# A fused linear-attention and mixture-of-experts kernel: other banks and engines for the first two half batches, plain loads for four v tiles, and a new written order

## The chip, the cores and the metric

The kernel runs on one core of a Trainium2 chip. The core has a matrix engine (TensorE, PE in the profile, with PEld for its weight loads), a vector engine (VectorE, DVE), an activation engine (ScalarE, ACT), a general one (GpSimd, POOL) and a queue engine (SyncE, SP), and 16 DMA engines that SP's, POOL's and ACT's transfers share. The metric is the device time of one execution in microseconds. Three runs before the change took 956.26, 956.44 and 956.66 us; the median, 956.44, is what the change is compared with.

## The reference, cut to what matters

```python
# q, k, v: (8, 8, 576, 64) float32; moe: x (4608, 512), w_gate (512, 8), w1 (8, 512, 1024), w2 (8, 1024, 512)
def phi(x): return np.where(x > 0, x, np.exp(x) - 1.0) + 1.0
q_p, k_p = phi(q), phi(k)
kv = einsum('bhsd,bhse->bhde', k_p, v);  z = sum(k_p, axis=2)
num = einsum('bhsd,bhde->bhse', q_p, kv)
den = einsum('bhsd,bhd->bhs', q_p, z)[..., None] + 1e-06
x = (num / den) transposed to (4608, 512)

P = exp(x @ w_gate - max)
for _ in range(8):                       # Sinkhorn: rows, then columns
    P /= P.sum(1, keepdims=True) + 1e-09
    P /= P.sum(0, keepdims=True) + 1e-09
    P *= N / E
out = sum over the experts e of P[:, e:e+1] * (maximum(x @ w1[e], 0) @ w2[e])
```

Every token goes through all eight experts, so nearly all of the arithmetic is in the two matrix products per expert.

## The kernel before, in words

**Two stages.** The front computes the attention and leaves its result x, turned (features on the partitions), in the fp16 tile xT. The experts follow: expert 0 with plain products (layer 1 at L618 with its relu at L622, layer 2 at L886), started while the front still runs, so that TensorE has work between the small attention products; the last four token groups of expert 0 and all of experts 1 to 7 with a seven-product scheme (L764/L769 for layer 1, L1024 for layer 2). There are nine groups g of 512 tokens. Layer 1 of a group has eight column blocks f0 to f7 of 128 columns of w1, each a sum over four chunks c of 128 features. For g = 0 the blocks f0 to f3 first do chunks 0 and 1, which half batch 0 yields, and later chunks 2 and 3, which half batch 1 yields.

**The front, by half batches.** `att(b, g)` handles four heads of one batch; there are 16 such half batches, n = 2b + g. Each has these steps:

- loads of k, q (one tile of two, `kqin`) and v (`vin`), L290, each tile with two buffers; for n = 0 and 1 on SP's queue, for n = 2 to 5 all on POOL's, from n = 6 on k and q on SP's and v on POOL's. `VC` is the set of half batches whose v is cast to fp16 by its load: from n = 2 on
- phi as max(x + 1, 1) at L319 (called t) and the minimum of that with exp at L322 (m) on VectorE, and exp at L306 on ScalarE
- v copied into a tile with a column of ones (the helper `copy`, L255 on ScalarE and L257 on VectorE)
- kv, 18 products (L351), and its scaled copy z (L363 on ScalarE, L365 on VectorE)
- q turned by TensorE (qT, L381) and copied out of PSUM
- num, in two parts of three and two row blocks (L407): the numerators, and the denominators as a further column. Then add 1e-6 (L417 on ScalarE, L419 on VectorE), the reciprocal (L422), and the quotient xn (L425, VectorE alone)
- xn turned by TensorE (xT, L440) and copied into the tile xT

Logits (L461) follow every two batches.

**PSUM.** The pool `kvps` has two pairs of banks, the tile `kv_ps`; kv, qT, num, xT and the logits all take turns in it. The pool `hqp` has two single banks, the tile `hq`, for layer 1 (blocks f0, f1, f4, f5, ... in turn; f2 and f3 of the first group use the two banks of layer 2). A bank is free again once its reader has run: for `hq`, the relu at L622.

**What sets the order.** The class `_Plan` takes tasks with costs, dependences and buffer groups. A written list, `order`, then gives for every engine and queue the numbers of its tasks in the order in which they are issued, up to the start of expert 1; behind that the planner picks by its costs. Each engine runs its tasks in that order and waits where an input or a buffer isn't ready. The costs in the code do not make the kernel wait; they only steer the planner where no list is written.

**The start.** SP issues the six loads of n = 0 and 1. POOL waits for v of n = 0 with a small copy, the gate (L342), then issues w1 of expert 0 in two halves, the loads of n = 2 and 3, w2 in two halves, and n = 4 and 5. TensorE runs 38 products on a tile of zeros (L536, `f_warm`): 30 tasks of one and four of two.

Of the kernel before, what the change touches and what calls it, by code (L numbers as in the profile page):

```python
# [11 lines left out]
FP16 = mybir.dt.float16  # L12
# [127 lines left out]
def kernel(  # L140
# [46 lines left out]
    VC = range(2, 2 * B)  # L187
# [19 lines left out]
    p_kv = S_.pool(2)  # L207

# [63 lines left out]
    def att(b, g):  # L272
# [6 lines left out]
        for nm, ten in (("k", k), ("q", q), ("v", v)):  # L279
# [17 lines left out]
            tin[nm] = fadd(("dma", 1.5 if n < 2 else 1.7), lambda _: None, deps=[ti], use=[gr], prio=pr, lat=2.6)  # L297
# [39 lines left out]
        tvv.append(fadd({"act": 1.15, "dve": 0.4 if n in VC else 0.76}, f_v, deps=[ta, tin["v"]],  # L337
# [36 lines left out]
        for j0, j1 in ((0, 5), (5, NJ)) if n < 2 else ((0, NJ),):  # L374
            gp = S_.grp(p_kv)

            def f_qt(_, gp=gp, j0=j0, j1=j1):
                gp["tile"] = pair_tile(FP16).rearrange("p b t -> p (b t)")[:, 0:(j1 - j0) * 2 * PW].rearrange(
                    "p (j h w) -> p j h w", h=2, w=PW)
                for j in range(j0, j1):  # L380
                    nc.tensor.transpose(gp["tile"][:, j - j0].rearrange("p h w -> p (h w)"),  # L381
                                        gt["q"]["tile"][:, j, 2:4, :].rearrange("p r d -> p (r d)"), ident)
# [15 lines left out]
        for i0, i1 in ((0, 3), (3, 5)):  # L398
# [25 lines left out]
            def f_xn(_, num=num, grd=grd, i0=i0, i1=i1, ni=ni):  # L424
                nc.vector.tensor_tensor(  # L425
                    out=gxn["tile"][:, i0:i1].rearrange("p i r h e -> p h (i r) e"), in0=num()[:, :, :, 0:D],
                    in1=grd["tile"][:, :, 0:2 * ni, None].broadcast_to([P, 2, 2 * ni, D]), op=ALU.mult)
# [4 lines left out]
            txn.append(fadd(("dve", 0.95 if ni == 3 else 0.69), f_xn, deps=[t2, txa], use=[gn, grd, gxn], prio=pr))  # L432
        for c0, c1 in ((0, 1), (1, 2)) if n < 2 else ((0, 2),):
            gx = S_.grp(p_kv)

            def f_xt(_, gx=gx, c0=c0, c1=c1):
                gx["tile"] = pair_tile(FP16)
                for c2 in range(c0, c1):
                    for i in range(5):
                        nc.tensor.transpose(gx["tile"][:, c2, 64 * js[i]:64 * js[i] + P],  # L440
                                            gxn["tile"][:, i, c2].rearrange("p h e -> p (h e)"), ident)

            def f_xc(e, gx=gx, c0=c0, c1=c1):
                copy(e, xT[:, 2 * g + c0:2 * g + c1, S * b:S * b + S], gx["tile"][:, c0:c1, 0:S])
# [89 lines left out]
    def f_warm(_, n=1):  # L534
        for _ in range(n):
            nc.tensor.matmul(yw[0], lhsT=warm[:, 0:P], rhs=warm, start=True, stop=True)  # L536
# [6 lines left out]
    for i in range(34):  # L543
        twa = add(("pe", 0.43 if i < 16 else 0.22), lambda e, n=2 if 12 <= i < 16 else 1: f_warm(e, n), deps=[twa],
# [10 lines left out]
    for b in range(1, B):  # L555
        att(b, 0)
        att(b, 1)
        if b == 1:
            w_t[0] += load_w2(0, prio=-96.5, parts=2, deps=[in_prev[0]])
# [562 lines left out]
    for d, k_ in zip(chain, chain[1:]):  # L1122
# [4 lines left out]
        485 515 525 573 1561 1563 1565 576 1083 1570 1567 1081 1107 1109 1206 1572 1574 1204 1230 1576 1232 1327 1329  # L1127
        1353
        pe 2 3 4 5 6 7 8 9 10 11 12 13 14 15 16 17 56 18 54 19 51 20 59 21 22 23 63 24 25 26 85 27 90 88 67 28 69 93
# [17 lines left out]
        sp 36 38 40 71 73 75 237 239 267 269 299 301 329 331 359 361 389 391 421 423 451 453 581 481 595 483 588 511  # L1147
        513 590 602 604 583 609 999 611 597 789 1001 791 1003 1005 1007 1009 1011 893 841 1122 843 1124 1126 945 895
        1128 947 1130 1132 1134 1245 1247 1249 1251 1253 1255 1257 1368 1370 1372 1374 1376 1378 1380 1491 1493 1495
        1497  # L1150
        act 42 43 49 77 52 78 84 64 116 117 619 621 625 627 146 629 147 128 631 623 633 155 165 161 183 184 169 642
# [11 lines left out]
        dve 44 45 46 47 57 79 55 80 81 60 61 82 62 65 66 86 91 89 68 70 94 95 98 96 99 100 102 104 118 120 119 121 123  # L1163
# [15 lines left out]
        dma 37 39 41 72 74 76 107 109 111 113 115 141 143 145 172 174 178 180 182 208 210 212 238 240 242 268 270 272  # L1179
# [39 lines left out]
```

## Time and profile before

| | |
|---|---|
| median of three runs | 956.44 us (956.26 to 956.66) |
| the profiled execution's own time | 956.11 us |
| its span, first to last instruction | 954.3 us |
| mean granted TensorE clock | 1.000 |
| TensorE busy | 944.9 us, 99% |
| VectorE, ScalarE, GpSimd busy | 770.4, 565.9, 161.2 us |
| load of k or q, SP's queue, issue to landing | 6.2 and 7.3 us (median), 576 KB each |
| load of k or q, POOL's queue | 10.3 and 11.3 us, 576 KB each |
| load of v with cast, POOL's queue | 8.3 us, 288 KB written |
| exp of k or q, L306 | 1.17 us, 128x1152 |
| t from fp32, L319, VectorE | 0.75 us, 128x1152 |
| copy of v on VectorE, fp16 to fp16 | 0.45 us; on ScalarE 1.15 us from fp32 |
| copy of qT, 128x1152 | 0.76 us on VectorE, 1.13 us on ScalarE |

How to read it: the profile is of one execution. A line such as "L306 ACT ACTIVATE e<-kqin" gives the source line, the engine, the operation and the tiles written and read. The name behind an arrow in brackets at the end of a line of the timeline is what ended the engine's idle time before it. TensorE's products overlap, so its busy time also holds products whose start is 0.216 us after the one before and whose record is 0.379 us long; gaps are best read from start to start.

### The profile page before, as it was taken

What the parts mean: (1) busy time and instruction counts of PE and PEld (TensorE: products, weight loads), DVE (VectorE), ACT (ScalarE), POOL (GpSimd) and SP (SyncE); (2) the same over time, 40 slices, a digit from 0 to 9 for tenths busy, and PEclk for the clock granted to TensorE, in tenths of its full rate; (3) what the DMA queues carried; (4) which work ended last, traced back from release to release, by engine and by line L of the source; (5) the groups of instructions that cost most, each with busy time, mean ns of one, the idle gap of its engine ahead of it and who ended that gap; (6) DMA issues with size and microseconds to landing.
All of it is one profiled execution on the core that took longest, in us unless ns stands there. A gap on an engine that the chain in (4) does not pass through costs nothing.

```text
span 954.3 us, 18433 instructions
## 1 busy us (share of the span) xinstructions
PE 944.9 (99%) x7096; PEld 643.8 (67%) x7096; DVE 770.4 (81%) x1528; ACT 565.9 (59%) x1024; POOL 161.2 (17%) x209
## 2 busy tenths in 40 slices
PE   8999999999999999999999999999999999999998
PEld 4565676466676667766676666766677666766676
DVE  7898988788887787888887787977877788877776
ACT  5799764765555555555555555555555555555551
POOL 4211000112112211221112211221112211111111
PEclk9999999999999999999999999999999999999999
DMA  9998783634255422544135431644125431425545
GB/s 305 276 252 224 197 252 117 100 78 99 68 149 111 112 67 61 112 111 100 57 115 113 102 89 45 147 105 107 57 67 108 111 98 56 139 78 160 151 105 133
DMA packets 110456, 117.67 MB, mean 123 GB/s; under 512 B 7840, under 2 KB 96544, under 8 KB 110368
## 3 DMA queue, kind: packets, MB, share of 16 engines
q1 hardware_dynamic: 81600, 90.33, 31.0%
q0 software_dynamic: 28368, 25.64, 16.6%
q8 instruction: 55, 0.90, 0.4%
q10 hardware_dynamic: 400, 0.52, 0.2%
q14 instruction: 33, 0.27, 0.1%
HBM read 119.69 MB, written 17.69 MB: 144 GB/s over the span
## 4 chain that ended last, share of the span: by engine, by line
PE 95%; DMA 2%; DVE 1%; ACT 1%; issue 0%; SPq 0%; DVEq 0%; ACTq 0%
PE ye L1024 34%; PE hq L764 20%; PE att L764 10%; PE ye L886 6%; PE Zye L1024 6%; PE Zye L764 5%; PE hq L769 4%; PE hq L618 3%; PE att L769 2%; DMA kqin<-in_k_dram 2%; PE Zye L769 1%; PE kv_ps L440 1%; PE kv_ps L351 1%; PE kv_ps L407 1%; PE kv_ps L381 1%; ACT e L306 1%
## 5 line engine op out<-in xcount | busy, mean ns | idle before, releaser
L1038 DVE SCALAR_TENSOR_TENSOR acc<-ye,P_sb,acc 128x256 f32<-128x256 f32 x620 | 266.5, 477 | 105.8 <-PE ye L1024 104.0
L1024 PEld LDWEIGHTS <-S 128*128 128x128 f16 x1984 | 194.1, 98 | 45.9 <-issue 0.2
L1048 POOL TENSOR_TENSOR acc<-acc,h 128x256 f32<-128x256 f32 x124 | 103.2, 849 | 603.3 <-ACT h L1045 603.2
L1024 PE MATMUL ye<-h,S 128*128 128x256 f16 x1488 | 192.8, 273 | 0.0
L1024 PEld LDWEIGHTS <-h 128*128 128x128 f16 x1488 | 145.6, 98 | 40.0 <-issue 0.2
L804 ACT ACTIVATE h<-hq 128x512 f16<-128x512 f32 x134 | 80.1, 598 | 139.5 <-PE hq L764 122.2
L764 PEld LDWEIGHTS <-W 128*128 128x128 f16 x896 | 87.7, 98 | 81.2
L764 PE MATMUL hq<-xs,W 128*128 128x512 f16 x448 | 133.2, 379 | 0.0
L764 PE MATMUL att<-xs,W 128*128 128x512 f16 x448 | 133.2, 379 | 0.0
L764 PE MATMUL hq<-xs,w 128*128 128x512 f16 x448 | 124.1, 379 | 0.4 <-DVE h L807 0.4
L764 PEld LDWEIGHTS <-w 128*128 128x128 f16 x672 | 65.8, 98 | 55.2 <-issue 0.6
L807 DVE CUSTOM_DVE_ANT_0 h<-att,s 128x512 f16<-128x512 f32 x126 | 86.5, 686 | 20.3 <-ACT s L791 19.8
L801 ACT ACTIVATE h<-Zye 128x512 f16<-128x512 f32 x134 | 80.2, 598 | 32.0 <-PE Zye L764 26.3
L784 ACT COPY Zye<-hq 128x512 f32<-128x512 f32 x134 | 77.7, 580 | 32.3 <-PE hq L764 23.1
L1045 ACT ACTIVATE h<-Zye,P_sb 128x256 f32<-128x256 f32 x124 | 52.4, 471 | 74.7 <-PE Zye L1024 74.5
L791 ACT COPY s<-hq 128x512 f32<-128x512 f32 x126 | 73.5, 584 | 35.3 <-PE hq L764 30.9
L807 DVE CUSTOM_DVE_ANT_0 h<-hq,s 128x512 f16<-128x512 f32 x126 | 86.4, 685 | 9.8 <-PE hq L764 9.3
L995 DVE TENSOR_TENSOR S<-h 128x1024 f16<-128x1024 f16 x124 | 85.3, 688 | 6.2 <-ACT h L804 6.2
L798 ACT COPY s<-att 128x512 f32<-128x512 f32 x126 | 74.5, 591 | 0.9 <-PE att L764 0.9
L886 PE MATMUL ye<-w,h 128*128 128x512 f16 x296 | 73.1, 379 | 0.0
L764 PE MATMUL Zye<-xs,w 128*128 128x512 f16 x224 | 66.6, 379 | 0.0
L1024 PE MATMUL ye<-h,h 128*128 128x256 f16 x496 | 64.3, 273 | 0.0
(121 smaller groups left out, 1077.0 us busy)
## 6 DMA issues: line engine op xcount, KB each, us to landing
xs<-xd SPq DMA_DIRECT2D x196, 256.0 KB, 4.0
w<-in_moe_w_dram POOLq DMA_DIRECT2D x48, 256.0 KB, 4.1
out_dram<-acc SPq DMA_DIRECT2D x67, 128.0 KB, 2.4
kqin<-in_k_dram SPq DMA_DIRECT2D x12, 576.0 KB, 6.2
kqin<-in_q_dram SPq DMA_DIRECT2D x12, 576.0 KB, 7.3
xs<-xd SPq DMA_DIRECT2D x49, 128.0 KB, 2.5
vin<-in_v_dram POOLq DMA_DIRECT2D x14, 288.0 KB, 8.3
xd<-xT SPq DMA_DIRECT2D x27, 128.0 KB, 3.4
```

The costliest lines, as they stand in the source:

```text
L764: nc.tensor.matmul(dst, lhsT=lhs(0, c), rhs=X(b)(c), start=(first and c == 0), stop=(c == 1), skip_group_check=True)
L784: nc.scalar.copy(out=Zt[1], in_=gX["tile"])
L791: nc.scalar.copy(out=gs2["tile"], in_=gX["tile"])
L798: nc.scalar.copy(out=gs5["tile"], in_=gR["tile"])
L801: nc.scalar.activation(out=hd(0, 0), in_=Zt[1], func=AF.Relu)
L804: nc.scalar.activation(out=hd(1, 0), in_=gX["tile"], func=AF.Relu)
L807: nc.vector._custom_dve(TENSOR_ADD_SAT, out=dst, in0=ps, in1=sb, s0=3.0e38, s1=0.0)
L886: nc.tensor.matmul(gy[tt]["tile"], lhsT=hx(f, P * tt, P), rhs=gw2["tile"][:, f, :], start=(f == 0), stop=(f == NFT - 1))
L995: nc.vector.tensor_tensor(out=gS[i]["tile"], in0=a0, in1=a1, op=op)
L1024: nc.tensor.matmul(bank(g_)[:, s, :], lhsT=lhs(s, kk), rhs=rhs(kk), start=(new and s == 0 and kk == 0), stop=(kk == 3), skip_group_check=True)
L1038: nc.vector.scalar_tensor_tensor(out=dst(), in0=bank(g_)[:, s, :], scalar=P_sb[:, gg, e:e + 1], in1=dst(), op0=ALU.mult, op1=ALU.add)
L1048: nc.gpsimd.tensor_tensor(out=dst(), in0=dst(), in1=gst["tile"], op=ALU.add)
```

## The change

It does five things; SP's and POOL's lists keep their first 30 us as they were.

- qT of half batches 0 and 1, and xT of half batch 0, are written to the single banks of `hqp` (`bank_tile`) and no longer to pairs of `kvps`. xT of half batch 1 stays in `kvps`.
- For half batches 0 and 1 `f_xn` can also run on ScalarE, as one multiply by the reciprocal for each row block and head (128x64 each). The order uses it once: for the two-block part of half batch 1, eight multiplies.
- `VC` starts at 6: v of half batches 2 to 5 comes as fp32, and the copy into the tile with the ones does the cast. These loads stay on POOL's queue.
- The 34 warm-up tasks have one product each: 34 in all. 17 of them are ahead of the first qT, where there were 20 products.
- The written order is new for all engines. At the front: VectorE does m of q ahead of m of k for n = 0; ScalarE takes the add of n = 0's three-block part (behind the cast of v, n = 1), both copies of qT n = 1, and one of the two copies of each xT of n = 0 and 1; VectorE takes the add of the two-block part. On TensorE the two-block num comes ahead of the three-block one, and num of n = 2 (two blocks) ahead of qT and kv of n = 3. VectorE takes the copies of qT n = 2 and xT n = 3, and z n = 3, from ScalarE; ScalarE takes the copies of v n = 3 and 5 and of xT n = 2. Further back TensorE has kv of half batch 14 right behind that of 13, and other tasks change between VectorE and ScalarE. The first load of w2 no longer depends on the last of n = 3's loads in the planner's eyes; POOL's list has it in the same place.

The planner's costs for loads and copies also change.

```diff
-    VC = range(2, 2 * B)
+    VC = range(6, 2 * B)
...
+    def bank_tile():
+        return hqp.tile([P, 1024], FP16, tag="hq", name="hq")
...
-            gp = S_.grp(p_kv)
+            gp = S_.grp(p_hq if n < 2 else p_kv)
...
-                gp["tile"] = pair_tile(FP16).rearrange("p b t -> p (b t)")[:, 0:(j1 - j0) * 2 * PW].rearrange(
-                    "p (j h w) -> p j h w", h=2, w=PW)
+                tl = bank_tile() if n < 2 else pair_tile(FP16).rearrange("p b t -> p (b t)")
+                gp["tile"] = tl[:, 0:(j1 - j0) * 2 * PW].rearrange("p (j h w) -> p j h w", h=2, w=PW)
...
-            def f_xn(_, num=num, grd=grd, i0=i0, i1=i1, ni=ni):
+            def f_xn(eng, num=num, grd=grd, i0=i0, i1=i1, ni=ni):
+                if eng == "act":
+                    for m in range(2 * ni):
+                        for h in range(2):
+                            nc.scalar.mul(out=gxn["tile"][:, i0 + m // 2, m % 2, h, :], in_=num()[:, h, m, 0:D],
+                                          mul=grd["tile"][:, h, m:m + 1])
+                    return
...
-            gx = S_.grp(p_kv)
+            gx = S_.grp(p_hq if n == 0 else p_kv)
...
-    def f_warm(_, n=1):
-        for _ in range(n):
-            nc.tensor.matmul(yw[0], lhsT=warm[:, 0:P], rhs=warm, start=True, stop=True)
+    def f_warm(_):
+        nc.tensor.matmul(yw[0], lhsT=warm[:, 0:P], rhs=warm, start=True, stop=True)
...
-            w_t[0] += load_w2(0, prio=-96.5, parts=2, deps=[in_prev[0]])
+            w_t[0] += load_w2(0, prio=-96.5, parts=2)
```

The order's first numbers on ScalarE and VectorE:

```diff
-        act 42 43 49 77 52 78 84 64 116 117 619 621 625 627 146 629 147 128 631 623 633 155 165 161 183 184 169 642
+        act 42 43 49 77 52 78 84 60 91 89 68 100 102 116 117 619 621 623 627 146 629 147 153 631 633 625 165 161 139
...
-        dve 44 45 46 47 57 79 55 80 81 60 61 82 62 65 66 86 91 89 68 70 94 95 98 96 99 100 102 104 118 120 119 121 123
+        dve 44 46 47 45 55 79 57 80 81 64 65 82 66 61 62 86 70 98 99 94 95 96 104 118 120 119 121 123 148 128 149 150
```

Here 116 and 117 are the exps of k and q for n = 2, 619, 621, ... the relus of layer 1's first group, 100 the part of xn n = 1, 91 and 89 the copies of qT n = 1, 68 and 102 copies of xT.

More of the change, by code (lines that the diff above doesn't have):

```diff
@@ L296, in att @@
             in_prev[0] = ti
-            tin[nm] = fadd(("dma", 1.5 if n < 2 else 1.7), lambda _: None, deps=[ti], use=[gr], prio=pr, lat=2.6)
+            tin[nm] = fadd(("dma", 1.55 if n < 2 else 2.0 if nm == "v" and n in VC else 1.7), lambda _: None, deps=[ti], use=[gr], prio=pr, lat=2.6)
         ge, gtt = S_.grp(p_e), S_.grp(p_t)
@@ L336, in f_v @@
             copy(e, gvv["tile"][:, :, :, 0:D], gin["v"]["tile"])
-        tvv.append(fadd({"act": 1.15, "dve": 0.4 if n in VC else 0.76}, f_v, deps=[ta, tin["v"]],
+        tvv.append(fadd({"act": 1.15, "dve": 0.46 if n in VC else 0.76}, f_v, deps=[ta, tin["v"]],
                         use=[gvv, gin["v"]], prio=pr))
@@ L431, in att @@
             t2 = fadd(("dve", 0.22), f_rd, deps=[t2], use=[grd], prio=pr)
-            txn.append(fadd(("dve", 0.95 if ni == 3 else 0.69), f_xn, deps=[t2, txa], use=[gn, grd, gxn], prio=pr))
+            txn.append(fadd({"dve": 0.95 if ni == 3 else 0.69, **({"act": 0.8 * ni} if n < 2 else {})}, f_xn, deps=[t2, txa], use=[gn, grd, gxn], prio=pr))
         for c0, c1 in ((0, 1), (1, 2)) if n < 2 else ((0, 2),):
-            gx = S_.grp(p_kv)
+            gx = S_.grp(p_hq if n == 0 else p_kv)
             def f_xt(_, gx=gx, c0=c0, c1=c1):
-                gx["tile"] = pair_tile(FP16)
+                gx["tile"] = bank_tile()[:, None, :] if n == 0 else pair_tile(FP16)[:, 0:c1 - c0]
                 for c2 in range(c0, c1):
                     for i in range(5):
-                        nc.tensor.transpose(gx["tile"][:, c2, 64 * js[i]:64 * js[i] + P],
+                        nc.tensor.transpose(gx["tile"][:, c2 - c0, 64 * js[i]:64 * js[i] + P],
                                             gxn["tile"][:, i, c2].rearrange("p h e -> p (h e)"), ident)
             def f_xc(e, gx=gx, c0=c0, c1=c1):
-                copy(e, xT[:, 2 * g + c0:2 * g + c1, S * b:S * b + S], gx["tile"][:, c0:c1, 0:S])
+                copy(e, xT[:, 2 * g + c0:2 * g + c1, S * b:S * b + S], gx["tile"][:, :, 0:S])
             t1 = fadd(("pe", 0.28 * (c1 - c0)), f_xt, deps=txn, acq=[gx], use=[gxn], prio=pr)
@@ L543 @@
     for i in range(34):
-        twa = add(("pe", 0.43 if i < 16 else 0.22), lambda e, n=2 if 12 <= i < 16 else 1: f_warm(e, n), deps=[twa],
+        twa = add(("pe", 0.43 if i < 26 else 0.22), f_warm, deps=[twa],
                   use=[gyw], prio=900.0, after=1.2 + 0.43 * min(i, 16) + 0.55 * max(i - 16, 0))
@@ L1126 @@
         pool 0 50 106 108 110 112 114 140 142 144 171 173 177 179 544 181 207 209 211 241 271 303 333 363 393 425 455
-        485 515 525 573 1561 1563 1565 576 1083 1570 1567 1081 1107 1109 1206 1572 1574 1204 1230 1576 1232 1327 1329
-        1353
-        pe 2 3 4 5 6 7 8 9 10 11 12 13 14 15 16 17 56 18 54 19 51 20 59 21 22 23 63 24 25 26 85 27 90 88 67 28 69 93
[12 rows of a table removed]
+        485 515 525 576 573 1561 1081 1570 1563 1572 1574 1565 1109 1107 1083 1567 1230 1206 1576 1204 1232 1327 1329
+        1353 1355
+        pe 2 3 4 5 6 7 8 9 10 11 12 13 14 15 16 17 18 56 54 19 51 20 21 22 63 59 23 24 25 88 90 26 27 85 28 29 67 69
[12 rows of a table added]
         1093 1163 1171 1173 1169 1100 1102 1105 1175 1110 1113 1177 1179 1181 1116 1185 1187 1183 1189 1260 1262 1119
@@ L1145 @@
         1391 1387 1320 1322 1325 1393 1330 1333 1395 1397 1399 1336 1403 1405 1401 1407 1411 1413 1339 1409 1417 1419
[1 row of a table removed]
-        sp 36 38 40 71 73 75 237 239 267 269 299 301 329 331 359 361 389 391 421 423 451 453 581 481 595 483 588 511
-        513 590 602 604 583 609 999 611 597 789 1001 791 1003 1005 1007 1009 1011 893 841 1122 843 1124 1126 945 895
-        1128 947 1130 1132 1134 1245 1247 1249 1251 1253 1255 1257 1368 1370 1372 1374 1376 1378 1380 1491 1493 1495
-        1497
-        act 42 43 49 77 52 78 84 64 116 117 619 621 625 627 146 629 147 128 631 623 633 155 165 161 183 184 169 642
[9 rows of a table removed]
[1 row of a table added]
+        sp 36 38 40 71 73 75 237 239 267 269 299 301 329 331 359 361 389 391 421 423 581 451 453 481 483 588 511 513
+        583 590 595 597 999 1001 1003 1005 789 602 1007 791 1009 604 1011 841 609 1122 611 1124 1126 945 1128 843 947
+        893 895 1130 1132 1134 1245 1247 1249 1251 1253 1255 1257 1368 1370 1372 1374 1376 1378 1380 1491 1493 1495
+        1497
+        act 42 43 49 77 52 78 84 60 91 89 68 100 102 116 117 619 621 623 627 146 629 147 153 631 633 625 165 161 139
[9 rows of a table added]
         1295 1293 1224 1229 1231 1301 1303 1305 1309 1307 1384 1386 1315 1390 1388 1321 1326 1328 1396 1398 1400 1404
         1402 1412 1414 1410 1418 1416 1347 1352 1354
-        dve 44 45 46 47 57 79 55 80 81 60 61 82 62 65 66 86 91 89 68 70 94 95 98 96 99 100 102 104 118 120 119 121 123
[13 rows of a table removed]
+        dve 44 46 47 45 55 79 57 80 81 64 65 82 66 61 62 86 70 98 99 94 95 96 104 118 120 119 121 123 148 128 149 150
[13 rows of a table added]
         1311 1313 1582 1243 1244 1316 1392 1317 1318 1323 1324 1319 1394 1342 1331 1332 1334 1335 1343 1344 1337 1338
[1 row of a table removed]
[1 row of a table added]
         dma 37 39 41 72 74 76 107 109 111 113 115 141 143 145 172 174 178 180 182 208 210 212 238 240 242 268 270 272
[4 rows of a table removed]
-        none 1 613 48 105 53 58 83 87 170 92 122 126 650 152 156 129 159 189 193 219 223 196 226 249 253 683 279 256
-        283 311 286 315 341 345 371 318 348 716 401 375 405 433 378 463 437 408 440 749 493 497 467 500 523 572 575
[4 rows of a table added]
+        none 1 170 613 48 105 53 58 83 87 92 122 126 650 129 152 156 159 189 193 196 219 223 226 249 253 683 279 283
+        256 311 286 315 341 345 318 371 348 716 375 401 378 433 405 437 408 463 440 749 493 497 467 523 500 572 575
         470 528 531 793 545 845 897 949 990 1013 1560 1136 1569 1259 1382
```

80 rows, old and new, of the table order are left out of this document.

## The prediction

> **What bounds the kernel now.** I read the page first (parts 1 and 2), then busy time by ten-microsecond stretches, then what TensorE waited for, then the timeline of the first 40 us.
>
> ```profile
> span 954.3 us, 18433 instructions
> PE 944.9 (99%) x7096; PEld 643.8 (67%) x7096; DVE 770.4 (81%) x1528; ACT 565.9 (59%) x1024; POOL 161.2 (17%) x209
> ```
>
> TensorE is busy 99% of the span, so time is won only where it idles or runs warm-ups. The next view (span of the stretch, then busy us of PE, PEld, DVE, ACT, POOL, granted clock, DMA share, GB/s) says where that is: in the first 40 us.
>
> ```profile
> 0.00:10.00 10.00, 8.51 (x49) 3.65 (x49) 5.04 (x18) 5.47 (x5) 2.88 (x9) 1.00 0.83 300
> 10.00:20.00 10.00, 8.44 (x87) 5.14 (x84) 8.80 (x21) 4.51 (x7) 6.41 (x9) 1.00 1.15 290
> 20.00:30.00 10.00, 9.33 (x94) 5.17 (x92) 8.38 (x14) 8.62 (x14) 4.74 (x7) 1.00 1.17 268
> 30.00:40.00 10.00, 9.47 (x71) 5.10 (x69) 8.50 (x17) 5.84 (x8) 0.65 (x2) 1.00 1.08 303
> 40.00:50.00 10.00, 10.00 (x132) 6.22 (x131) 9.16 (x19) 8.36 (x15) 1.31 (x2) 1.00 1.01 288
> ...
> 70.00:80.00 10.00, 9.69 (x116) 5.90 (x115) 8.91 (x20) 9.20 (x15) 1.41 (x2) 1.00 0.96 258
> 80.00:90.00 10.00, 9.76 (x109) 5.93 (x108) 8.26 (x19) 8.83 (x16) 0.00 (x0) 1.00 0.77 209
> ```
>
> There the DMA queues are full (share above 1) and the loads land one after another. What matters is what the first useful stretch waits for, on ScalarE:
>
> ```profile
> 13.33 0.26 ACT L417 ACTIVATE rden<-kv_ps,eps 128x8 f32<-128x8 f32 x1
> 18.77 1.16 ACT L306 ACTIVATE e<-kqin 128x1152 f16<-128x1152 f32 x1 [5.18 <-DVE rden L422]
> 21.25 1.16 ACT L306 ACTIVATE e<-kqin 128x1152 f16<-128x1152 f32 x1 [1.31 <-DMA kqin<-in_q_dram]
> 22.32 2.29 ACT L622 ACTIVATE h<-hq 128x512 f16<-128x512 f32 x4
> ```
>
> ScalarE lies idle 5.2 us while VectorE alone finishes half batches 0 and 1. Then the exp of the third half batch's q starts at 21.25 on its landing, and the first relu of layer 1 (L622) stands behind it. That relu ends at 22.90; layer 1's fifth column block needs the bank it frees, and starts at 22.95. From there the timeline has TensorE idle at 27.6 (0.56 us), 29.4 (0.39), 29.9 (0.31) and 31.7 (0.55), in all 1.81; after 32.2 only at 75.6 (0.48), 88.8 (0.41) and 111.0 (0.16), 1.05 in all, up to the end of attention.
>
> **The change part by part.** Names: k, q, v of half batch n; t and m (L319, L322), kv (L351), z (L363/365), qT (L381), num (L407), xn (L425), xT (L440). Loads land as before for half batches 0 and 1: k 4.78, q 6.26, v 7.76, k 9.27, q 10.78, v 12.25.
>
> *Half batches 0 and 1.* Until 11.9 VectorE does the same work (m of k after m of q, which kv n0 covers: it waits for v's cast, 8.94, and z stands behind the exp that ends at 10.46, as before). Num n0 is done at 11.8. VectorE: add, reciprocal, m q n1 (ends 12.85), the small xn 13.45. The large half's add is now ScalarE's, queued behind v n1's cast: 13.33-13.60; so reciprocal 13.87, large xn 14.84. This is 0.2 us later than the 14.64 of before, and z n1 follows at 15.18 (was 14.97). But qT n1 in layer 1's banks goes out at 12.9 without waiting for a kv_ps pair, and its copies sit on the idle ScalarE (512 and 640 columns between the rows 0.59 for 512 and 1.12 for 1152: 0.59 and 0.70, done 14.8). So xT n0 runs at 14.9 (was 15.61), num n1 at 15.45 (was 16.59), and xT n0 is copied on two engines by 16.1 (was 17.04). ScalarE's share of xn n1 is eight multiplies of 128x64. No row has that shape. The nearest is L363, 128x130, 374 ns, two of which start 0.25 apart: between 8x0.2 = 1.6 (the gap shrinks with the columns) and 8x0.37 = 3.0. I take 0.25 and 2.1: reciprocal 16.5, multiplies to 18.6. VectorE's half ends 17.9. xT n1 18.6-19.1, copies 19.8: 1.3 us ahead of the 21.06 of before.
>
> *What that lead is worth.* The blocks f0 to f3 of layer 1 (column blocks of 128) end at 21.6 instead of 22.9. The fifth needs relu f0, which in the new ScalarE order still stands behind both exps of n2; q n2 comes by the POOL queue behind w1, and nothing in front of it moved (SP has the same six loads, POOL the gate and w1 ahead of it). It lands at 21.22 again, exp to 22.4, relu 22.9, block five at 22.93. The whole lead becomes idle TensorE time: worth 0, between 0 and 1.3. I take 0 since the landing is a row. For the same reason a slow ScalarE costs little: at 3.0 us for the multiplies the exp of n2's q would end at 22.8, 0.4 late.
>
> *Loads of v without cast, n2 to n5.* Before, v lands 1.28 after q (25.47 to 26.75), while a full fp32 load behind another takes 1.45. So +0.17 each, between 0 and 0.2: v n3 at 27.05, the halves of w2 at 29.6 and 32.2 (were 29.30, 31.88). v's copy grows on VectorE from 0.46 to 0.75 (L319, the same shape from fp32) for n2 and n4; n3's and n5's go to ScalarE at 1.15 (its cast row).
>
> *Half batches 2 and 3, from 22.93.* TensorE: block five 0.86 to 23.79, qT n2 0.50 (m ready 23.3), block six to 25.16, kv n2 0.72, blocks seven and eight to 27.61. z n2 ends 27.46 on VectorE, so num n2's small half goes to 27.85. qT n3 waits for m q n3 (28.14): idle 0.32, ends 28.68. kv n3 takes the kv_ps pair of that num, which xn frees only at 29.14: idle 0.48, to 29.78. Num n2's large half waits for the copy of qT n3 (29.83): 0.08, to 30.21; num n3 waits for z n3 (30.40): 0.22, to 30.66. Then four layer-2 steps (L886, 0.86 each), num n3 and both xT run on without a wait (w2's second half is wanted at 33.3, there 32.2; xn n3 ends 34.4, wanted 35.0), to 35.60. Idle in all 1.10 where it was 1.81. The same set of work ended at 36.3 before: **0.7 us won**. Bounds: 1.8 won if all of it went, and 0 if the waits come to before's 1.81.
>
> *From 36 us to the end of attention.* VectorE has less queued ahead than before: summed by these durations, mostly 0 to 4 us less at the steps up to half batch 8, because 3.4 us went to ScalarE's idle time. ScalarE is level after 20 us: about 15.6 us leaves it and 13.7 comes. I see TensorE go on without a wait to about 64 us. The three later waits (1.05) can all go, or three more of the mean 0.45 may come (+1.35); in the middle, and nearest to before's own count, I take -0.1. Layer work after attention is bound by TensorE at 100% in every stretch, and the order there moves VectorE and ScalarE tasks only: 0, at most the 0.4 it idles between 200 and 300 us.
>
> *Warm-ups.* 38 become 34, 17 instead of 20 ahead of the first qT. The first twelve start 0.427 apart, all later ones 0.216, and no later matmul of before is at the slow rate, though from 12.9 to 16.6 there are only 1.06 us of matmuls that are no transposes. The new schedule has 1.5 us in its emptiest such stretch. I cost this at 0; the cover is that TensorE isn't the limit before 22.9.
> The Trainium skill (TensorE: Matmul & The Clock Gate, Parts 1 and 4) says that an idle window of about 3.4 us halves the clock and that transposes don't count as busy for it. By it, fewer warm-ups between transposes could bring the slow rate back, the case costed among the rivals; the row above speaks against it here.
>
> *Sum.* -0.7 - 0.1 = -0.8 us. The profiled execution took 956.11 (span 954.3 and 1.8 around it), 0.33 under the median of 956.44. So span 953.5, and for the median **955.6 us**. About 0.2%, 1.9 us, is what a measurement of this kernel can tell from no change, so this is "no change".
>
> **The rivals.**
> *The lead is kept (faster).* The trace's packets show one 16 KB fetch of TensorE's program at 18.11 that holds one of the 16 DMA engines for 0.99 us, and q n2 landed 2.5 us after k instead of 1.45. The new program reaches that fetch only when xT n1 is let go, by my schedule 18.6; past about 19.2 it would miss q n2, which would land near 20.2, and up to 1.0 of the lead stays: -1.8, with the later waits gone -2.8 (953.6). Against: v n2 and all behind it still meet the lagging engine.
> *Two pairs of kv_ps are too few (slower).* In the new order num of one half batch stands ahead of kv of the next, so a pair waits for VectorE's xn; above this cost 0.48. Before's waits average 0.45, and 6 more between 64 and 120 us, where half batches 12 to 15 are nested, give +2.7 - 0.7 = +2.0 (958.4). That is where it decides: six. For it: VectorE is 83 to 98% busy there. Against: its shorter queue.
> *The clock falls back (slower, if less).* A slow stretch like the first, 1.34 to 6.30, that falls on layer 1 loses half of its 5.0 us: 2.5, less 1.3 of slack where it lies ahead of 22.9: +1.2 to +2.5, less the 0.7: 956.9 to 958.2.
> *It does nothing measurable.* New waits equal old ones in both stages: 956.4.
>
> **How the numbers follow.** My forecast with its own range 954.6 to 956.3: 0.43. Lead kept: 0.20, with at least one later wait gone and so past -1.9. Pairs: 0.24, of which 0.20 with six waits or more, since I followed the order by hand only to 64 us. Clock: 0.04. Nothing: 0.09. The last two and the rest lie within the bound. So faster 0.20, same 0.60, slower 0.20. The 8-in-10 range runs from 953.7 (lead kept, later waits gone) to 958.3 (six waits).
>
> **What would show it.** Right: xT n1 copied before 20.2; ScalarE busy between 13.6 and 18.8; block five still at 22.9, with a TensorE gap of about 1.3 before it; half batches 2 and 3 done near 35.6; v n3 landing near 27.0. Wrong: q n2 landing early, a multiply of 128x64 above 0.37, TensorE gaps on kv_ps between 64 and 120 us, or matmul starts 0.427 apart after 8 us.

## The result

The changed kernel takes 953.95 us (median of 18 runs, 953.7 to 954.35), and the kernel before, timed beside it, 956.01 (18 runs, 955.04 to 961.66). The ratio is 0.9976, with a 95% interval of 0.9968 to 0.9984. That is 2.3 us less than before (1.5 to 3.1): a small gain, just past the 0.2% set as the bound. (The two medians alone differ by 2.1 us.) The forecast was 955.6 (-0.8 us) and "no change"; its 8-in-10 range, 953.7 to 958.3, held the time, the forecast's own range, 954.6 to 956.3, did not. The profiled execution took 954.18 us with a span of 952.4, where before had 956.11 and 954.3: 1.9 us less.

The page of the changed kernel, its span and TensorE's line:

```profile
span 952.4 us, 18434 instructions
PE 943.2 (99%) x7092; PEld 643.9 (68%) x7092; DVE 771.0 (81%) x1527; ACT 566.6 (59%) x1030; POOL 161.5 (17%) x209
```

Busy time in stretches of the changed kernel (span of the stretch, then PE, PEld, DVE, ACT, POOL, granted clock, DMA share, GB/s), from 10 us on, as in the prediction:

```profile
10.00:20.00 10.00, 8.91 (x98) 5.36 (x93) 7.70 (x18) 8.10 (x19) 6.93 (x9) 1.00 1.13 284
20.00:30.00 10.00, 8.46 (x79) 4.55 (x79) 8.89 (x16) 9.32 (x14) 4.73 (x6) 1.00 1.12 314
30.00:40.00 10.00, 9.93 (x90) 5.86 (x84) 8.70 (x16) 5.64 (x9) 0.72 (x1) 1.00 1.12 367
...
70.00:80.00 10.00, 10.00 (x115) 5.93 (x113) 9.70 (x24) 9.57 (x15) 0.99 (x2) 1.00 0.95 264
80.00:90.00 10.00, 10.00 (x110) 6.21 (x110) 9.08 (x20) 9.72 (x14) 1.41 (x2) 1.00 0.85 236
```

From 10 to 20 us ScalarE is busy 8.10 us instead of 4.51, which is mostly the work moved to it. From 20 to 30 TensorE is busy less than before (8.46 against 9.33): it finishes layer 1's first blocks sooner and then waits. From 30 us on it is nearly always busy, and in 70 to 90 us always, where before had 0.55 us of idle time.

ScalarE's timeline of the changed kernel (start, duration, then what), which answers to the four lines of before:

```profile
13.87 0.27 ACT L420 ACTIVATE rden<-kv_ps,eps 128x12 f32<-128x12 f32 x1
14.19 1.18 ACT L258 COPY qpT<-hq 128x512 f16<-128x512 f16 x2
...
17.20 1.75 ACT L431 ACTIVATE xn<-kv_ps,rden 128x64 f16<-128x64 f32 x8 [0.50 <-DVE rden L422]
19.39 0.64 ACT L258 COPY xT<-kv_ps 128x576 f16<-128x576 f16 x1 [0.43 <-PE kv_ps L449]
19.93 1.16 ACT L309 ACTIVATE e<-kqin 128x1152 f16<-128x1152 f32 x1
21.58 1.16 ACT L309 ACTIVATE e<-kqin 128x1152 f16<-128x1152 f32 x1 [0.49 <-DMA kqin<-in_q_dram]
22.65 1.55 ACT L630 ACTIVATE h<-hq 128x512 f16<-128x512 f32 x3
```

ScalarE's idle stretch of 5.2 us is filled. But the exp of n2's q still starts on its landing (21.58; in this execution v n0 landed 0.57 us later than in before, and q n2 0.34 later), and relu f0 still stands behind it. So the fifth block of layer 1 starts at 23.28, in before at 22.95. TensorE's two longest waits between 20 and 36 us in the changed kernel, for that relu and later for the buffer that xn frees:

```profile
23.28 1.02 PE L626 MATMUL hq<-xT,w 128*128 128x512 f16 x4 [0.85 <-ACT h L630]
...
29.67 0.69 PE L354 MATMUL kv_ps<-vv,t 64*128 64x130 f16 x18 [0.48 <-DVE xn L434]
```

Where the 1.9 us between the two traces are, by TensorE's idle gaps (start to start of its instructions, less the usual spacing): the fifth block 0.33 later; half batches 2 and 3 wait 1.20 instead of 1.81 us (-0.61); the three later waits of attention are gone (-1.05); and a wait of 0.57 us at 238 us, in the expert layers, is gone. Sum -1.90. The list leaves out a wait of 0.22 us at 173 us, which every trace with the old order has there and no trace with the new one; and it is good to some 0.2 us only. Counted back from the last product, TensorE is ahead of before by 1.22 us at 130 us, 1.42 at 200 and 1.94 from 250 on. The changed kernel has no gap of 0.15 us or more from 36 us to 930.

### The profile page after: what moved, and what is told of

Its sections match the earlier page's. It is cut to its first block, busy times and chain, and to the rows that moved or that the text cites. A ratio compares the mean times of both kernels' runs of the same rounds, so it can differ in the third digit from the quotient of the medians.

```text
span 952.4 us, 18434 instructions
## 1 busy us (share of the span) xinstructions
PE 943.2 (99%) x7092; PEld 643.9 (68%) x7092; DVE 771.0 (81%) x1527; ACT 566.6 (59%) x1030; POOL 161.5 (17%) x209
## 3 DMA queue, kind: packets, MB, share of 16 engines
q1 hardware_dynamic: 81600, 90.33, 31.1%
## 4 chain that ended last, share of the span: by engine, by line
PE 96%; DMA 2%; DVE 1%; SPq 0%; ACT 0%; POOL 0%; issue 0%; POOLq 0%
PE ye L1032 34%; PE hq L772 20%; PE att L772 10%; PE ye L894 7%; PE Zye L1032 6%; PE Zye L772 5%; PE hq L777 4%; PE hq L626 3%; PE att L777 2%; DMA kqin<-in_k_dram 2%; PE Zye L777 1%; PE kv_ps L354 1%; PE kv_ps L449 1%; PE kv_ps L410 1%; PE kv_ps L384 1%; PE kv_ps L470 0%
## 5 line engine op out<-in xcount | busy, mean ns | idle before, releaser
L1053 ACT ACTIVATE h<-Zye,P_sb 128x256 f32<-128x256 f32 x124 | 52.5, 471 | 77.7 <-PE Zye L1032 75.6
L792 ACT COPY Zye<-hq 128x512 f32<-128x512 f32 x134 | 77.7, 580 | 31.7 <-PE hq L772 25.0
L1032 PE MATMUL ye<-w,h 128*128 128x256 f16 x496 | 64.3, 273 | 0.0
```

What stands on the lines that cost most here:

```text
L792: nc.scalar.copy(out=Zt[1], in_=gX["tile"])
L1032: nc.tensor.matmul(bank(g_)[:, s, :], lhsT=lhs(s, kk), rhs=rhs(kk), start=(new and s == 0 and kk == 0), stop=(kk == 3), skip_group_check=True)
```

## The experiments

All were timed beside the kernel before, whose median was 956.31 beside the first four, 956.49 beside the next four, 956.61 beside three more and 956.48 beside the last. In what follows "new order" is the changed kernel's, "old order" that of before. What theories A to D stand for is said in each expectation.

### The two halves of the change

**first_half_alone** has the new code and order for half batches 0 and 1, then the old order, with v cast from n2 on:

```diff
-    VC = range(6, 2 * B)
+    VC = range(2, 2 * B)
...
-        act ... 68 100 102 116 117 619 621 623 627 ...
+        act ... 68 100 102 116 117 619 621 625 627 ...
```

> The first half alone: other banks and the ScalarE multiplies for half batches 0 and 1 with the new order up to there, then the old order and the old v loads (cast from half batch 2 on). Theory A (the lead is void, because the relu of layer 1 stands behind the exp of the third half batch's q, and the rest of the new order is what pays): xT of half batch 1 is ready about 1 us earlier, block five of layer 1 starts where it did (22.9 to 23.3), and the time is that of the kernel before within 0.3 us. Rival B (the shorter queue of VectorE from the first half is what removes the later waits): 1 to 2 us under the kernel before.

**rest_alone** is its complement: the old code and order for half batches 0 and 1, the new order behind them.

```diff
-            gp = S_.grp(p_hq if n < 2 else p_kv)
+            gp = S_.grp(p_kv)
...
-            gx = S_.grp(p_hq if n == 0 else p_kv)
+            gx = S_.grp(p_kv)
...
-        act 42 43 49 77 52 78 84 60 91 89 68 100 102 116 117 619 621 623 627 ...
+        act 42 43 49 77 52 78 84 64 116 117 619 621 623 627 ...
```

> The rest alone: half batches 0 and 1 as in the kernel before (pairs of kv_ps, VectorE for xn and the copies, the old order up to there), then the new order, and plain v loads for half batches 2 to 5. Theory A: all of the gain, 1.7 to 2.2 us under the kernel before, with block five at about 22.95 and no wait of TensorE between 40 and 120 us. Rival B: little of it, 0 to 0.7 us under the kernel before, with waits on kv_ps between 64 and 120 us.

Measured: the first half alone 956.21 us, ratio 0.9999 (0.9991 to 1.0007). The rest alone 954.29, ratio 0.998 (0.9971 to 0.9988). So the rest carries all of the gain, and the turned q and x in layer 1's banks with ScalarE's normalization carry none that can be seen. Where its order changes over, the first half alone waits from 28 to 33 us as before does (0.55, 0.41, 0.31 and 0.54 us), so it doesn't pay for the joint. Why the lead is worth nothing shows in what TensorE waited for between 20 and 36 us (times waited in all, how often, longest). In the first half alone:

```profile
PE hq L626 <- ACT h L630: 1.2, 1, 1.2
```

TensorE is done early with four blocks and then waits 1.2 us for relu f0, which stands behind the exp of the late q. In the rest alone the same wait is 0.4 us. The lead turned into a wait at the place that the prediction named.

### Parts of the first half

**xn_vector** gives xn n1's part back to VectorE:

```diff
-        act ... 68 100 102 116 ...
+        act ... 68 102 116 ...
-        dve ... 94 95 96 104 118 ...
+        dve ... 94 95 96 100 104 118 ...
```

> The changed kernel with the eight ScalarE multiplies of half batch 1 given back to VectorE (one multiply of 0.69 us behind the 0.94 one). xn n1 then ends at about 19.1 instead of 18.95. Theory A: xT of half batch 1 about 0.2 us later, block five unmoved, the time that of the changed kernel within 0.2 us. Rival B (each us of the first half counts): 0.2 us slower at most, so only a larger difference would speak for neither.

**v_cast_from_2** is the changed kernel with `VC = range(2, 2 * B)`, so that v of n2 to n5 is cast by its load again.

> The changed kernel with the cast back in the v loads of half batches 2 to 5. Theory A: v n3 lands 0.3 to 0.4 us earlier, but kv n3 waits for a pair of kv_ps and for m, not for v: the time is that of the changed kernel within 0.3 us. Rival C (the cast loads take the DMA engines longer, and the plain loads are a part of the gain): 0.5 to 1 us slower than the changed kernel, with the loads of half batches 4 and 5 landing later.

**relu_first** puts relu f0 ahead of the exp of q n2:

```diff
-        act ... 102 116 117 619 621 ...
+        act ... 102 116 619 117 621 ...
```

> The changed kernel with the first relu of layer 1 ahead of the exp of q n2 on ScalarE, so that block five need not wait for that load. Theory A (the loads pace this stretch, so a lead is taken back at the next step): block five starts at about 22.3 instead of 23.3, but qT n2 still waits for m q n2 (23.7) and qT n3 for m q n3 (28.5); TensorE's waits grow by what block five wins, and the time is that of the changed kernel within 0.2 us. Rival B (the wait for relu f0 itself costs): 0.7 to 1.0 us under the changed kernel.

Measured: 953.98, 954.06 and 954.08 us (ratios 0.9975, 0.9976 and 0.9976, each with an interval of about 0.001 to either side). None can be told from the change itself. In v_cast_from_2 the v of n3 landed 1.27 us after its q, without the cast (xn_vector) 1.44 us: the plain load is 0.17 us longer, as costed, and hidden. In relu_first the fifth block no longer waits, but the wait comes back at once in front of qT n2. TensorE's timeline of relu_first:

```profile
20.63 2.54 PE L626 MATMUL hq<-xT,w 128*128 128x512 f16 x11
23.79 0.68 PE L384 MATMUL kv_ps<-ident,t 128*128 128x128 f16 x9 [0.63 <-DVE t L325]
```

Eleven matmuls of layer 1 run without a break, then qT waits for t, which is made from the same late load. So the bound there is q n2's landing, and this order of the work in front of it meets it too.

### The warm-ups

**few_warm** issues only the first 17 of the 34 warm-ups, so none behind the first qT, where the transposes are:

```diff
-    def f_warm(_):
-        nc.tensor.matmul(yw[0], lhsT=warm[:, 0:P], rhs=warm, start=True, stop=True)
+    def f_warm(_, on=True):
+        if on:
+            nc.tensor.matmul(yw[0], lhsT=warm[:, 0:P], rhs=warm, start=True, stop=True)
...
-        twa = add(("pe", 0.43 if i < 26 else 0.22), f_warm, deps=[twa],
+        twa = add(("pe", 0.43 if i < 26 else 0.22), lambda e, on=(i < 17): f_warm(e, on), deps=[twa],
```

> The changed kernel without the last 17 warm-up products (17 are left, all ahead of the first qT). Theory A (the clock needs no filler here): matmul starts stay 0.216 apart for 512 columns after 7 us, the time is that of the changed kernel within 0.3 us. Rival by the Trainium skill's page TensorE: Matmul & The Clock Gate (transposes do not count as busy, an idle window of about 3.4 us halves the clock): layer 1 starts with products 0.427 apart, up to 2.5 us lost there, 0.5 to 2.5 us slower than the changed kernel.

Measured: 954.36 us, ratio 0.9976 (0.9968 to 0.9985): by the medians 0.4 us above the change, by the ratios nothing. But the clock did fall, as the rival said. The stretch of few_warm in which it did:

```profile
10.00:20.00 10.00, 6.85 (x79) 5.02 (x74) 7.78 (x18) 7.46 (x17) 6.42 (x9) 0.83 1.15 306
```

The mean granted clock of 0.83 over 10 us is 3.4 us at one half (0.17 x 10 / 0.5; the clock's own record has 3.413 us at 0.5, from 15.62 us on). The change, with its 17 fillers, has 1.00 there. So it is the fillers between the transposes that keep the clock up here, and 17 are enough. Without them the slow stretch ended at 19.03 us, and TensorE reached the wait for relu f0 only 0.2 us later than in the change (the wait is 0.88 us, in the change 1.01); this is why it cost so little. The Trainium skill (TensorE: Matmul & The Clock Gate, Parts 1 and 4) says that an idle window of about 3.4 us halves the clock and that transposes don't count as busy in the same way. The run fits the first: from 12.2 us to the fall TensorE was busy for 1.6 us, 0.8 of it without transposes, and the half clock lasted 3.41 us. Whether the transposes counted, no run here shows.

### The wait at 238 us

In all four profiles with the old order's VectorE list there (before, first_half_alone, before_again, before_w_late) TensorE waits 0.56 or 0.57 us at 237 to 239 us. In before, VectorE and TensorE (timelines):

```profile
236.32 1.20 DVE L995 TENSOR_TENSOR S<-h 128x1024 f16<-128x1024 f16 x1
237.44 0.68 DVE L807 CUSTOM_DVE_ANT_0 h<-hq,s 128x512 f16<-128x512 f32 x1
```

```profile
238.17 1.02 PE L764 MATMUL hq<-xs,w 128*128 128x512 f16 x4 [0.40 <-DVE h L807]
```

TensorE waits for the h that frees a bank, and h stands behind a sum S that takes 1.20 us, where other S take 0.68. Three runs ask why, and attention_order further down settles it.

**late_w2_issue**, in the changed kernel, moves two of expert 2's weight issues to the place of the third, near 236.7 us:

```diff
-        ... 1570 1563 1572 1574 1565 1109 1107 1083 1567 1230 1206 1576 1204 ...
+        ... 1570 1563 1565 1109 1107 1083 1567 1230 1206 1572 1574 1576 1204 ...
```

> The changed kernel with two of the issues of expert 2's w2 by GpSimd moved from about 200 us to about 236 us, beside the third that stands there, as the kernel before has them (233.8 to 237.6). Theory A (GpSimd's issues stretch VectorE's S from 0.68 to 1.20 us there, and TensorE waits 0.57 for the relu behind it): a TensorE gap of 0.4 to 0.6 near 236 us and 0.4 to 0.6 us slower than the changed kernel. Rival B (the gap at 238 of the kernel before comes from the rest of the order): no gap there, the time within 0.2 us of the changed kernel.

Measured: 954.13 us, 0.9976 (0.9968 to 0.9985), no wait, S at 0.68. It settles little: no S ran while the three issues did (236.7 to 238.9).

**before_w_late**, in the kernel before, moves the issues behind GpSimd's accumulations:

```diff
-        ... 1206 1572 1574 1204 1230 1576 1232 ...
+        ... 1206 1204 1230 1232 1572 1574 1576 ...
```

> The kernel before, with one change: GpSimd issues expert 2's last three weight loads behind its accumulations of 234 to 239 us instead of between them. Theory A: no issue overlaps a sum S any more, both sums near 234 and 236 us take 0.68 to 0.75 us instead of 1.20, the TensorE wait of 0.57 us at 238 us goes, and the time is 0.4 to 0.6 us under the kernel before. Theory B: S may be shorter, but a wait of at least 0.3 us stays, and the time is that of before within 0.2 us.

Measured: 956.98 us, 1.0004 (0.9994 to 1.0013). The wait stays at 0.56, and both sums stay stretched, now without an issue beside them. VectorE and GpSimd in before_w_late:

```profile
234.77 1.22 DVE L995 TENSOR_TENSOR S<-h,S 128x1024 f16<-128x1024 f16 x1
...
236.70 1.20 DVE L995 TENSOR_TENSOR S<-h 128x1024 f16<-128x1024 f16 x1
```

```profile
233.13 2.30 POOL L1048 TENSOR_TENSOR acc<-acc,h 128x256 f32<-128x256 f32 x2 [15.37 <-ACT h L1045]
236.62 1.85 POOL L1048 TENSOR_TENSOR acc<-acc,h 128x256 f32<-128x256 f32 x2 [1.19 <-ACT h L1045]
```

The accumulations moved up and took the issues' place. One accumulation alone is 0.72 to 0.74 us; two take 2.30 and 1.85 here. The instructions one by one: the accumulation of 236.62 ends at 237.34, and S, begun at 236.70, ends 0.55 us later, most of its usual 0.68. So S stood still while GpSimd worked. The reverse shows in the changed kernel at 247.65 us, VectorE first and then GpSimd:

```profile
247.65 0.68 DVE L1003 TENSOR_TENSOR S<-h 128x1024 f16<-128x1024 f16 x1
```

```profile
247.04 1.87 POOL L1056 TENSOR_TENSOR acc<-acc,h 128x256 f32<-128x256 f32 x2 [8.13 <-ACT h L1053]
```

S keeps its 0.68, and the second of these two accumulations, begun 0.08 us after S, takes 1.18. The Trainium skill (SBUF — State Buffer, Who interferes with whom) says that VectorE with two SBUF inputs and a GpSimd instruction that reads SBUF exclude each other, and that the one issued first holds the port; both traces agree, with about 0.5 us for the loser. What held the first S of before (234.39 to 235.61) isn't settled. Weight issues ran beside it until 235.24, and an accumulation is on record only from 235.26; but over the 14 traces 239 VectorE instructions of this kind and shape ran beside weight issues alone, and none took over 0.69 us.

**h_first**, in the kernel before, swaps h with that S in VectorE's list:

```diff
-        ... 1221 1226 1227 1222 1299 ...
+        ... 1221 1226 1227 1299 1222 ...
```

> The kernel before with one swap in VectorE's list: the h that frees the bank for which TensorE waits at 238 us goes ahead of the second sum S there. Theory B (VectorE's order makes this wait: the stretched S stands ahead of h, whatever stretches it): h runs at 236.3 to 237.0 us instead of 237.4 to 238.1, the wait of 0.57 us at 238 us is gone, S may still take up to 1.2 us, and the time is 0.4 to 0.6 us under that of before, which is within what the interval can tell. Theory D (h could not have run earlier, or TensorE needs that S just as soon): a wait of 0.3 us or more stays between 236 and 241 us, and the time is that of before.

Measured: 956.28 us, 0.9993 (0.9984 to 1.0003). VectorE in h_first:

```profile
235.33 1.22 DVE L995 TENSOR_TENSOR S<-h,S 128x1024 f16<-128x1024 f16 x1
...
237.25 0.68 DVE L807 CUSTOM_DVE_ANT_0 h<-hq,s 128x512 f16<-128x512 f32 x1
237.85 0.68 DVE L995 TENSOR_TENSOR S<-h 128x1024 f16<-128x1024 f16 x1
```

The wait at 238 us is gone, by one swap, though the first S is still stretched; the trace has TensorE 0.56 us earlier behind it. The time alone couldn't show half a microsecond. So h behind S is one condition of this wait. It isn't what the change took away: the changed kernel's VectorE list has the same `1226 1227 1222 1299`, S directly ahead of h. The other condition is the stretch, and attention_order, below, tells the two apart.

### The waits of attention

**before_again** is the kernel before, once more.

> The kernel before, unchanged, for a second trace. Theory A: the gap at 238 us (0.57) comes again, since the order makes it; the waits at 75.6 and 88.8 us (0.48 and 0.41) come or go with how late the loads of the first half batches land, so that an execution whose block five starts later has fewer of them. Rival B: both come again whatever the loads do.

Measured: 956.62 us, 1.0002 (0.9991 to 1.0012). Its waits in attention are not those of the first trace: none at 75.6 and 88.8, but one of 1.36 us that ends at 104.0. All profiles side by side: from 36 to 130 us TensorE's gaps of 0.15 us or more sum to 1.05, 0.17, 1.52, 1.23 and 1.73 us in the five with the old order there (before, first_half_alone, before_again, before_w_late, h_first): 1.14 in the mean. With the new order they are zero in all nine. In the last three of the five, the large wait is the same. ScalarE and TensorE in before_again:

```profile
100.74 1.16 ACT L306 ACTIVATE e<-kqin 128x1152 f16<-128x1152 f32 x1 [1.63 <-DMA kqin<-in_q_dram]
101.81 1.14 ACT L255 COPY vv<-vin 128x1152 f16<-128x1152 f16 x1
102.85 1.11 ACT L255 COPY xT<-kv_ps 128x1152 f16<-128x1152 f16 x1
```

```profile
104.01 0.69 PE L351 MATMUL kv_ps<-vv,t 64*128 64x130 f16 x18 [1.20 <-ACT xT L255]
```

ScalarE waits 1.63 us for q of n14; the copies of v and xT stand behind that exp, and kv needs the pair that the xT copy frees. The load is issued late because of SyncE's list. SyncE's issues in before_again, then in the changed kernel:

```profile
87.85 0.37 SPq L290 DMA_DIRECT2D kqin<-in_k_dram  x1
91.03 0.34 SPq L672 DMA_DIRECT2D xd<-acc  x1
91.42 1.54 SPq L290 DMA_DIRECT2D kqin<-in_q_dram  x1
```

```profile
87.44 0.37 SPq L293 DMA_DIRECT2D kqin<-in_k_dram  x1
87.86 0.47 SPq L293 DMA_DIRECT2D kqin<-in_q_dram  x1
89.71 0.34 SPq L680 DMA_DIRECT2D xd<-acc  x1
```

In the old list (`481 595 483`) a store of acc, which waits 3.1 us for VectorE's result, stands between k and q of n14, so q is issued 3.6 us after k; in the new one (`481 483 588`) 0.4 us after. It landed at 100.2 to 100.7 us in the three profiles with the large wait, at 99.1 in the two of the old order without it, and at 93.2 to 94.6 with the new order. That is 4.4 to 7.6 us later than with the new order, so the late issue, 3.6, is not all of it; and a landing at 99.1 cost no large wait. No run moves that store alone, so this is read from 14 traces and not tested by itself; and the 0.48 and 0.41 of the first trace have other causes that I didn't follow to a load.

**attention_order** takes the new order to the end of attention, with all loads, and then the old lists of TensorE, ScalarE and VectorE. The three lists change over between 142 and 172 us:

```diff
-        1353 1355
+        1353
...
-        966 968 974 1014 1016 972 976 ...
+        966 974 972 968 1014 976 1016 ...
```

> The changed kernel's code, its loads, its GpSimd list (weight issues included) and its order of TensorE, ScalarE and VectorE up to the end of the attention part; from there (about 142 us on TensorE, 150 to 172 us on the other two) TensorE, ScalarE and VectorE take the order of the kernel before. Theory A (the 0.57 us wait of before at 238 us came from GpSimd issuing expert 2's weight loads while VectorE summed S): the new GpSimd list issues five of them at 199 to 203 us, so S stays near 0.68 us, the wait stays away and the time stays at the changed kernel's, 954.0 +-0.3. Theory B (the wait came from VectorE's old order around 234 us, in which two sums S stand ahead of h): S near 0.68 us, but a wait of some tenths is back at 236 to 238 us, and the time is 954.3 to 954.6. Theory C (order and weight issues together, the old order placing S on an issue): with the old order S meets the one issue left at 236.7 us, is stretched to about 1.2 us, and the wait is back at 0.3 to 0.6 us. All: no TensorE wait between 36 and 150 us.

Measured: 956.87 us, 1.0002 (0.9993 to 1.001), and against what any theory said, no gain. Attention has no wait, as expected of the new order. But at the change-over TensorE waits 0.51, 0.86 and 0.33 us (166 to 174 us), and then 0.94 at 240, in all 2.64; without these the time would be 954.2, by this sum. The last of them has another cause than the wait of before: ScalarE's copy (Zye, L792) is late, behind an h that waited 3.0 us for GpSimd. Here half of one order joined to half of another cost as much as the new order had won.

At 238 us there is no wait, as theory A said, though VectorE's list there is that of before. VectorE in attention_order:

```profile
235.82 0.68 DVE L1003 TENSOR_TENSOR S<-h 128x1024 f16<-128x1024 f16 x1
236.42 0.68 DVE L815 CUSTOM_DVE_ANT_0 h<-hq,s 128x512 f16<-128x512 f32 x1
```

The first S begins at 234.44 us, in before at 234.39. Neither sum is stretched, and h ends at 237.11 instead of 238.12. GpSimd, with the changed kernel's list, begins its first accumulation there at 236.29 and its weight issue at 237.73, when the first S has ended and the second has started. So the wait of before needs both: h behind the sums, and sums that GpSimd's work stretches by some 1.05 us together. Either cure is enough (h_first, attention_order); the changed kernel has the second.

### An attempt to do better

**fill_waits** fills the new order's waits at 29.0 and 30.6 us with layer-2 steps, VectorE normalizing as in xn_vector:

```diff
-        pe ... 134 157 154 130 164 638 636 160 ...
+        pe ... 134 157 638 154 130 636 164 160 ...
-        act ... 629 147 153 631 633 625 ...
+        act ... 629 147 625 153 631 633 ...
```

> The changed kernel with VectorE's normalization as in xn_vector, and three moves near 29 us: the first layer-2 block ahead of kv of half batch 3, the second ahead of that half batch's num, and ScalarE's relu f3 ahead of the cast of v n3, so that the first block's input is ready at 28.2 us. Theory A (what is waited for there is buffers and VectorE, and layer 2's blocks of 0.87 us can fill it): the waits of 0.65 and 0.23 us are filled, TensorE is 0.5 to 0.9 us earlier from 36 us on, and the time is 953.1 to 953.6. Theory B (the half batches' chain through VectorE sets the pace, so that the wait only moves): a wait of 0.6 us or more shows up again before 45 us, and the time stays at 954.0 +-0.2.

Measured: 955.25 us, 0.9987 (0.9979 to 0.9996): by the ratios 1.1 us slower than the change. TensorE in fill_waits:

```profile
29.67 1.02 PE L894 MATMUL ye<-w,h 128*128 128x512 f16 x4 [0.80 <-DMA w<-in_moe_w_dram]
...
33.29 0.52 PE L410 MATMUL kv_ps<-kvz,qpT 128*128 128x130 f16 x6 [0.42 <-DVE xn L434]
...
34.26 0.73 PE L449 MATMUL kv_ps<-ident,xn 128*128 128x128 f16 x10 [0.45 <-DVE xn L434]
```

The first layer-2 step now waits for its weights (in the change it starts at 31.1 us and finds them there), and two waits for VectorE's xn come behind it (0.59 and 0.61 us from start to start). The waits moved and grew.

## Why the prediction was right or wrong

- **The lead of half batches 0 and 1, worth 0:** right. xT n1 was copied at 20.1 instead of 21.06, and the fifth block came no sooner (first_half_alone 0.9999; relu_first only moves the wait). The rival "the lead is kept" didn't happen: the fetch of TensorE's program that it hung on came at 18.29 us (before 18.11), and q n2 landed no earlier (21.56, before 21.22).
- **ScalarE's eight multiplies, 2.1 us:** they took 1.75, 0.2 apart; like the moved part as a whole (xn_vector), without effect.
- **Loads of v, +0.17 and hidden:** right, by landings (1.44 us behind q against 1.27) and by v_cast_from_2.
- **Half batches 2 and 3, -0.7:** the mechanism held, with idle time 1.20 where 1.10 was worked out, so -0.61. The step wrong in it is kv n3's wait, 0.65 instead of 0.48, while the 0.08 ahead of num n2 didn't come.
- **"From 36 us to the end of attention", -0.1:** this is the term that failed, in size. All waits went, 1.05 against the first trace, 1.14 against the mean of five. I had this case among the bounds ("can all go") but took a value near before's count; the middle of the two bounds, -1.05 and +1.35, would have been +0.15, so -0.1 was chosen and not worked out. Two things were not looked at. SyncE's list is part of the "order anew", and I had followed the POOL and SP queues only for the first loads; k and q of n14 with a store between them could be read from the diff (that this store makes the large wait of three traces is likely but not tested, and what made the three small ones of the first trace stays open). And I took waits of one execution as fixed, though they hang on when loads land and differ from one profile to the next.
- **"Layer work after attention", 0:** failed too, by the 0.57 us at 238 us and 0.22 at 173. I called the stretches bound by TensorE at 100% and took none of the 0.4 that the row left idle as winnable. And the order there does not move VectorE and ScalarE tasks only, as I wrote: GpSimd's weight issues and accumulations move too, and with its new list the stretch of VectorE's sums, and so the wait at 238 us, is gone (attention_order).
- **Warm-ups, 0:** right for this change. The reading behind it, that the row speaks against the clock falling, went too far: before had some fillers in that stretch, and with the last 17 of the change gone the clock does fall (few_warm).
- **The rival of two kv_ps pairs too few** didn't occur: no wait of 0.15 us from 36 us on.

- **The 8-in-10 range** held the time, 953.95, by luck: its low end, 953.7, stood for the lead being kept, which didn't happen.

-0.61, -1.14 and -0.57 make -2.3 us, which is what the ratio gives, and with the 0.22 at 173 us -2.5; the ratio's interval is 1.5 to 3.1, so the closer match means nothing. The forecast's -0.8 had the first term and a tenth of the others.

## What to carry to other kernels

When a written order is replaced, follow every queue through all stages, the DMA issuers' too: a store between two loads of one list delayed the issue of the second by 3.6 us, and in three of five traces TensorE then waited 1.1 to 1.6 us (read from traces, not tested). A wait can need two things at once, here a place in one engine's list and another engine's work, and then one swap that cures it doesn't say which of the two a change removed. Take a wait that hangs on a load's landing from several executions before giving it a price. And work freed ahead of a late load is worth nothing until the load itself is earlier.

## What the runs showed of the hardware

- With the 17 fillers between transposes and short matmuls gone, the granted clock fell to 0.5 for 3.41 us.
- A VectorE sum of two SBUF tensors and a GpSimd accumulation exclude each other: 1.20 instead of 0.68 us for the sum if GpSimd was first (before_w_late), 1.18 instead of 0.73 for the accumulation if VectorE was (the changed kernel at 247.65 us). Weight issues of GpSimd alone stretched none of 239 such VectorE instructions.
- The same load took very different times: q of n14 needed 6.6 to 9.5 us from issue to landing in the five traces with the old order, where a store is issued ahead of it, and 5.4 to 6.0 in the nine with the new. Which of the transfers beside it made the difference wasn't tested.
